# Loading the first feed-forward weights in smaller pieces, with GpSimd's v product among the loads

## The chip, the cores and the metric

The kernel runs on one core of a Trainium2 chip. The metric is the device time of one execution in microseconds (us). In the normal (fast) state, the granted TensorE clock was 0.99 to 1.00.

Engine names are those of the profile: PE is TensorE, PEld its weight loads, DVE VectorE, ACT ScalarE, POOL GpSimd, SP SyncE. L90 is line 90 of the kernel; the changed kernel's line numbers are one higher than those of the kernel before in most places.

## The reference, cut to what matters

A linear attention with decay (4 batches, 8 heads, 768 steps, head size 64) feeds a gated feed-forward layer:

```python
for t in range(S):
    state = gamma * state + einsum('bhd,bhe->bhde', k[:, :, t], v[:, :, t])
    y[:, :, t] = scale * einsum('bhd,bhde->bhe', q[:, :, t], state)
x = y.transpose(0, 2, 1, 3).reshape(B * S, H * D)          # 3072 x 512
gate = 1 / (1 + exp(-(x @ w_gate)))                        # w_gate, w_val: 512 x 1536
out = (gate * (x @ w_val)) @ w_out                         # w_out: 1536 x 512
```

The kernel cuts the steps into chunks of 128 and the 3072 rows of `x` into six tiles of 512. Of the feed-forward width, one "row block" is 128 of the 1536 columns of the gate and value weights.

## The kernel before

Nearly every load is issued by GpSimd, which also converts float32 to bfloat16 on the way. These loads pass through one queue in the order in which they are issued. The helpers for the weights, in which one call loads the gate and value weights of two row blocks:

```python
def load_gate_val(s):
    cols = slice(s * 256, (s + 1) * 256)
    for dst, w in ((wg, moe_w_gate), (wv, moe_w_val)):
        nc.gpsimd.dma_start(out=dst[:, :, cols],
                            in_=w.rearrange("(kk p) n -> p kk n", p=128)[:, :, cols])

def scale_run(a, eng):        # the "v product": v times its decay, bfloat16 out
    vsr[a] = const.tile([128, H, 2, D], BF16, name=f"vsr{a}")
    eng.tensor_tensor(vsr[a], runs(vr[a]), tabr[:, a]..., op=ALU.mult)
```

The order in which GpSimd gets its work is the order of these calls (all other engines' work is cut):

```python
vr[1] = load_run(v, 1, F32, "vr", nc.gpsimd)   # the "v run": chunks 2 and 3
...                                            # a mask
load_gate_val(0)                               # row blocks 0 and 1
load_gate_val(1)                               # 2 and 3
load_gate_val(2)                               # 4 and 5
scale_run(1, nc.gpsimd)                        # the v product, 1.9 us
...
extend_taby(3)                                 # a table, 1.0 us
for s in range(3, NFF // 2):
    load_gate_val(s)                           # row blocks 6 to 11
causal = ...; extend_taby(4); extend_taby(5)   # a mask and two tables
for s in range(4):
    load_out(s)                                # w_out in four parts
load_chunk(4)                                  # k, q, v of attention chunk 4
load_chunk(5)
...
```

`load_chunk(g)` issues k, q and v of a chunk. PE transposes k and q of chunks 4 to 7 itself when it reaches them; from chunk 8 a transposing load does it. PE's program is fixed, so a late load is a wait of PE.

Of the kernel before, what the change touches and what calls it, by code (L numbers as in the profile page):

```python
# [17 lines left out]
def kernel(  # L18
# [50 lines left out]
    def load_chunk(g):  # L69
        load_kq(g)  # L70
        load_v(g)
# [10 lines left out]
    wg = wpool.tile([128, KT, D_FF], BF16, name="wg")  # L82
    wv = wpool.tile([128, KT, D_FF], BF16, name="wv")
    wo = wpool.tile([128, NFF, D_MODEL], BF16, name="wo")

    def load_gate_val(s):
        cols = slice(s * 256, (s + 1) * 256)
        for dst, w in ((wg, moe_w_gate), (wv, moe_w_val)):
            nc.gpsimd.dma_start(out=dst[:, :, cols],
                                in_=w.rearrange("(kk p) n -> p kk n", p=128)[:, :, cols])  # L90

    def load_out(s):
        nc.gpsimd.dma_start(out=wo[:, s * 3:(s + 1) * 3, :],
                            in_=moe_w_out.rearrange("(n p) d -> p n d", p=128)[:, s * 3:(s + 1) * 3, :])
# [44 lines left out]
    def tab_y(c):  # L139
        first = c if c in taby else c - 1  # L140
        return taby[first][:, :, (c - first) * C:(c - first + 1) * C]
# [6 lines left out]
    def extend_taby(c):  # L148
        nc.gpsimd.tensor_tensor(tab_y(c), tab_y(c - 3), gup.unsqueeze(2).to_broadcast([128, NP, C]), op=ALU.mult)
# [5 lines left out]
    def bank(shape, dt=F32):  # L155
        return pf.tile(shape, dt, tag="ff", name="ff")
# [85 lines left out]
    def x_cols(t, kk, lo, hi):  # L242
        if hi - lo == 512:
            return xT[t][:, :, kk, :]
        half = lo // 256
        return xT[t][:, half, kk, lo - half * 256:hi - half * 256]
# [11 lines left out]
    def runs(t):  # L258
        return t.rearrange("x h (j d) -> x h j d", j=2)
# [19 lines left out]
    def scale_run(a, eng):  # L279
        vsr[a] = const.tile([128, H, 2, D], BF16, name=f"vsr{a}")  # L280
        eng.tensor_tensor(vsr[a], runs(vr[a]), tabr[:, a].unsqueeze(3).to_broadcast([128, H, 2, D]), op=ALU.mult)  # L281
# [20 lines left out]
    def inter_run(g, first=True):  # L302
        a, c = divmod(g, 2)
        if first:
            y[g] = bank([128, NP, C])
        if g > 0:
            for p in range(NP):
                nc.tensor.matmul(y[g][:, p, :], zbd[g - 1][:, p, :], qT[a][:, p, :, c * D:(c + 1) * D],
                                 start=(first and p == 0), stop=not first, skip_group_check=True)
# [25 lines left out]
    def sum_run(g):  # L335
        if g == 0:
            nc.vector.tensor_copy(new_za(g), zz[g])
        else:
            nc.vector.tensor_tensor(new_za(g), za[g - 1], zz[g], op=ALU.add)
# [42 lines left out]
    def up(t, n1, lo=0, hi=512, between=None):  # L382
        if t not in hT:
            hT[t] = ffn.tile([128, NFF, 512], BF16, tag="hT", name="hT", bufs=2)
        ps = []
        for w in (wg, wv):
            u = bank([128, 512])
            for kk in range(KT):
                nc.tensor.matmul(u[:, lo:hi], w[:, kk, n1 * 128:(n1 + 1) * 128], x_cols(t, kk, lo, hi),  # L389
                                 start=(kk == 0), stop=(kk == KT - 1))  # L390
            ps.append(u)
        if between:
            between()
        gs = ffn.tile([128, 512], F32, tag="gs", name="gs")
        nc.scalar.activation(gs[:, lo:hi], ps[0][:, lo:hi], AX.Sigmoid)  # L395
        nc.vector.tensor_tensor(hT[t][:, n1, lo:hi], gs[:, lo:hi], ps[1][:, lo:hi], op=ALU.mult)  # L396

    def up_columns(t, n1s, lo, hi, rows=1):
        if t not in hT:
            hT[t] = ffn.tile([128, NFF, 512], BF16, tag="hT", name="hT", bufs=2)  # L400
        n = hi - lo
        us = [bank([128, 512]), bank([128, 512])]
        for row in range(rows):
            for w, u in zip((wg, wv), us):
                for i, n1 in enumerate(n1s):
                    for kk in range(row * KT // rows, (row + 1) * KT // rows):
                        nc.tensor.matmul(u[:, i * n:(i + 1) * n], w[:, kk, n1 * 128:(n1 + 1) * 128],  # L407
                                         x_cols(t, kk, lo, hi), start=(kk == 0 and (rows == 1 or i == 0)),
                                         stop=(kk == KT - 1), skip_group_check=rows > 1)
        ps = [u[:, :len(n1s) * n] for u in us]  # L410
        gs = ffn.tile([128, 512], F32, tag="gs", name="gs")
        g = gs[:, :len(n1s) * n]
        nc.scalar.activation(g, ps[0], AX.Sigmoid)
        nc.vector.tensor_tensor(hT[t][:, n1s[0]:n1s[-1] + 1, lo:hi], g.rearrange("p (i n) -> p i n", n=n),  # L414
                                ps[1].rearrange("p (i n) -> p i n", n=n), op=ALU.mult)
# [18 lines left out]
    def keep_on(n, u):  # L434
        for _ in range(n):
            nc.tensor.matmul(u, ident, ident4, start=True, stop=True)  # L436
# [24 lines left out]
    for i in range(2):  # L461
        half = maskr[i * D:(i + 1) * D]
        nc.gpsimd.affine_select(half, half, pattern=[[-1, 2], [1, 2], [2, D]], base=0, channel_multiplier=-2,  # L463
                                compare_op=ALU.is_ge, fill=0.0)
    maskr2 = maskr.rearrange("x j i p -> x (j i p)").unsqueeze(1).to_broadcast([128, 2, 4 * D])
    load_gate_val(0)
    load_gate_val(1)
    load_gate_val(2)
    scale_run(1, nc.gpsimd)
    warm = bank([128, 4, 128])  # L470
    keep_on(9, warm)
    kT[0], qT[0], kT[1], qT[1] = (new_run_T() for _ in range(4))
# [22 lines left out]
    masks_run(1, 0)  # L495
    masks_run(1, 1)
    keep_on(2, warm)
    up_columns(0, range(0, 2), 0, 256)
    inter_run(2)
    state_run(1)  # L500
    sum_run(2)
    state_out(2, za[2])
    sum_run(3)
    extend_taby(3)
    for s in range(3, NFF // 2):
        load_gate_val(s)
    causal = const.tile([128, 128], F32, name="causal")
    nc.gpsimd.memset(causal, 1.0)
    nc.gpsimd.affine_select(causal, causal, pattern=[[1, 128]], base=0, channel_multiplier=-1,
# [1 line left out]
    causal4 = causal.unsqueeze(1).to_broadcast([128, NP, 128])  # L511
    extend_taby(4)
    extend_taby(5)
    for s in range(4):
        load_out(s)
    load_chunk(4)
    load_chunk(5)
    for load in (load_kq, load_v):
# [99 lines left out]
```

## Time and profile before

| | before |
|---|---|
| time, median (range), 3 runs | 230.01 us (229.79 to 231.38) |
| profiled execution | 229.69 us, span 228.0 |
| PE busy | 220.3 us, 97% of the span |
| v run of chunks 2 and 3 landed | 13.29 us after the start of the span |
| q of chunk 5 landed | 42.81 us |

PE is almost always busy, so a change can only gain where PE waits, and it loses wherever it makes PE wait longer. What GpSimd does (in its timeline the columns are start, duration, engine, line, operation, output<-input, and in brackets the idle time before it):

```profile
12.44 0.79 POOL L89 DMA_DIRECT2D wv<-in_moe_w_val_dram  x1
13.46 1.90 POOL L281 TENSOR_TENSOR vsr<-vr,tabr 128x1024 bf16<-128x1024 f32 x1 [0.23 <-ACT qkT L272]
15.32 1.04 POOL L149 TENSOR_TENSOR taby<-taby,gup 128x512 f32<-128x512 f32 x1
16.30 0.81 POOL L89 DMA_DIRECT2D wg<-in_moe_w_gate_dram  x1
```

From the end of the sixth weight issue (13.23) to 16.30, GpSimd issues nothing. Whether the queue notices depends on what is still in it. It did not notice here, as the stretches of two microseconds show (columns: stretch and length, busy time of PE, PEld, DVE, ACT and POOL with instruction counts, granted clock, DMA share, and GB/s in the last column):

```profile
16.00:18.00 2.00, 1.68 (x53) 1.39 (x56) 1.60 (x3) 0.93 (x2) 2.00 (x4) 1.00 1.43 193
18.00:20.00 2.00, 1.99 (x57) 1.45 (x44) 1.67 (x4) 1.19 (x3) 2.00 (x3) 1.00 1.44 199
20.00:22.00 2.00, 1.98 (x20) 1.62 (x18) 1.46 (x3) 1.26 (x4) 1.93 (x5) 1.00 1.46 195
...
24.00:26.00 2.00, 2.00 (x13) 1.04 (x11) 0.69 (x1) 0.81 (x2) 2.00 (x4) 1.00 1.48 204
```

(The DMA share is that of 16 engines; it exceeds 1 because the recorded times of an engine's packets overlap.)

### The profile page before, as it was taken

To read this page: it belongs to the slowest core of one execution; us is meant where nothing else is said; L and a number is where in the kernel's file an instruction comes from. 1 tells how busy PE (TensorE), PEld (TensorE's weight loads), DVE (VectorE), ACT (ScalarE), POOL (GpSimd) and SP (SyncE) were. 2 spreads that over 40 slices of the span, in tenths; PEclk is the share of its full clock that TensorE was granted. 3 is DMA by queue.
4 is the path that set the end of the run, shared out by engine and by line. 5 is a ranking of instruction groups with operands and counts; after the bars stand their busy time and mean duration, and the time that the engine had idled before them with its cause. 6 is when DMAs were issued, how large, how long until landed. Compare 5 with 4: busy or idle time off the path is not lost.

```text
span 228.0 us, 4533 instructions
## 1 busy us (share of the span) xinstructions
PE 220.3 (97%) x1815; PEld 119.4 (52%) x1815; DVE 117.9 (52%) x224; ACT 87.4 (38%) x162; POOL 78.6 (34%) x106
## 2 busy tenths in 40 slices
PE   4979999999999999999999999999999999999994
PEld 1558544557886455445445445454445454444444
DVE  5496433278877817359617358627267530343301
ACT  4695332563452422532522432523432412433221
POOL 7999956760814527090710090810000000000000
PEclk9999999999999999999999999999999999999999
DMA  7999999999999999899892499992410012100022
GB/s 138 214 183 196 198 205 197 177 256 205 141 155 65 171 186 146 189 140 155 78 185 84 110 136 151 100 155 92 113 26 3 0 49 92 46 0 0 4 92 92
DMA packets 77669, 28.09 MB, mean 123 GB/s; under 512 B 64208, under 2 KB 73296, under 8 KB 77648
## 3 DMA queue, kind: packets, MB, share of 16 engines
q0 software_dynamic: 55440, 16.78, 66.0%
q1 hardware_dynamic: 21536, 10.69, 24.4%
q10 hardware_dynamic: 672, 0.33, 0.5%
q8 instruction: 14, 0.23, 0.4%
q14 instruction: 7, 0.06, 0.1%
HBM read 28.31 MB, written 6.29 MB: 152 GB/s over the span
## 4 chain that ended last, share of the span: by engine, by line
PE 90%; DMA 5%; POOL 1%; ACT 1%; DVE 1%; issue 0%; DVEq 0%
PE ff L389 50%; PE ff L425 26%; PE ff L407 5%; DMA wv<-in_moe_w_val_dram 3%; PE ff L235 2%; PE ff L186 2%; DMA vr<-in_v_dram 2%; PE ff L198 1%; PE ff L444 1%; PE z L204 1%; PE ff L165 1%; DVE vsr L281 1%; ACT qkT L167 0%; POOL vr L79 0%; POOL maskr L463 0%; ACT zbd L210 0%
## 5 line engine op out<-in xcount | busy, mean ns | idle before, releaser
L396 DVE TENSOR_TENSOR hT<-gs,ff 128x512 bf16<-128x512 f32 (+1 forms) x70 | 44.7, 648 | 57.8 <-PE ff L389 53.4
L389 PE MATMUL ff<-xT,wg 128*128 128x512 bf16 (+1 forms) x280 | 67.7, 364 | 0.0
L389 PE MATMUL ff<-xT,wv 128*128 128x512 bf16 (+1 forms) x280 | 67.6, 364 | 0.0
L395 ACT ACTIVATE gs<-ff 128x512 f32<-128x512 f32 (+1 forms) x70 | 39.5, 567 | 68.0 <-PE ff L389 62.0
L425 PE MATMUL ff<-wo,hT 128*128 128x512 bf16 x276 | 62.2, 379 | 0.0
L389 PEld LDWEIGHTS <-wv 128*128 128x128 bf16 x280 | 27.3, 98 | 29.0 <-DMA wv<-in_moe_w_val_dram 0.3
L425 PEld LDWEIGHTS <-hT 128*128 128x128 bf16 x276 | 26.3, 98 | 30.5
L389 PEld LDWEIGHTS <-wg 128*128 128x128 bf16 x280 | 26.9, 98 | 27.8
L430 ACT COPY ob<-ff 128x512 f32<-128x512 f32 x23 | 13.5, 587 | 49.0 <-PE ff L425 44.8
L253 DVE TENSOR_TENSOR xT<-ff,taby 128x512 bf16<-128x512 f32 x20 | 12.9, 686 | 21.8 <-PE ff L235 21.8
L559 POOL COPY gate<-qkX 1x1 bf16<-1x1 bf16 x7 | 1.2, 178 | 57.7 <-DMA qkX<-qn 57.7
L66 POOL DMA_DIRECT2D kn<-in_k_dram x20 | 17.8, 892 | 6.2 <-DMA qkX<-kn 1.5
L61 POOL DMA_DIRECT2D vf<-in_v_dram x20 | 18.3, 913 | 2.3 <-DMA wo<-in_moe_w_out_dram 1.0
L67 POOL DMA_DIRECT2D qn<-in_q_dram x20 | 17.9, 893 | 2.1 <-DMA wo<-in_moe_w_out_dram 1.6
L210 ACT CAST zbd<-za 64x256 bf16<-64x256 f32 x38 | 15.4, 405 | 7.1 <-DVE za L222 3.1
L177 DVE TENSOR_TENSOR vs<-vf,tabv 128x512 bf16<-128x512 f32 x20 | 13.6, 687 | 7.4 <-DMA vf<-in_v_dram 7.4
L191 DVE TENSOR_TENSOR stA<-ff,causal 128x512 bf16<-128x512 f32 x20 | 13.6, 681 | 0.0
L192 DVE TENSOR_TENSOR stB<-ff,causal 128x512 bf16<-128x512 f32 x20 | 13.6, 681 | 0.0
L436 PE MATMUL ff<-ident 128*128 128x512 bf16 x15 | 5.8, 532 | 3.0 <-POOL ident masks.py:199 3.0
L407 PE MATMUL ff<-xT,wg 128*128 128x256 bf16 x56 | 7.3, 272 | 0.7 <-DMA wg<-in_moe_w_gate_dram 0.7
L407 PE MATMUL ff<-xT,wv 128*128 128x256 bf16 x56 | 7.3, 273 | 0.3 <-DMA wv<-in_moe_w_val_dram 0.3
L414 DVE TENSOR_TENSOR hT<-gs,ff 128x512 bf16<-128x512 f32 x7 | 4.7, 685 | 3.9 <-PE ff L407 2.8
(86 smaller groups left out, 150.9 us busy)
## 6 DMA issues: line engine op xcount, KB each, us to landing
out_dram<-ob SPq DMA_DIRECT2D x23, 256.0 KB, 2.0
vf<-in_v_dram POOLq DMA_DIRECT2D x20, 256.0 KB, 5.4
kn<-in_k_dram POOLq DMA_DIRECT2D x20, 128.0 KB, 5.3
qn<-in_q_dram POOLq DMA_DIRECT2D x20, 128.0 KB, 5.5
wg<-in_moe_w_gate_dram POOLq DMA_DIRECT2D x6, 256.0 KB, 8.0
wv<-in_moe_w_val_dram POOLq DMA_DIRECT2D x6, 256.0 KB, 8.5
wo<-in_moe_w_out_dram POOLq DMA_DIRECT2D x4, 384.0 KB, 10.4
kr<-in_k_dram POOLq DMA_DIRECT2D x2, 256.0 KB, 5.6
```

Source lines behind the costliest of these rows:

```text
L61: nc.gpsimd.dma_start(out=vf[g], in_=src(v, g))
L66: nc.gpsimd.dma_start(out=kn[g], in_=src(k, g))
L67: nc.gpsimd.dma_start(out=qn[g], in_=src(q, g))
L177: nc.vector.tensor_tensor(vs[g], vf[g], tabv[:, g % NCH, :].unsqueeze(2).to_broadcast([C, H, D]), op=ALU.mult)
L191: nc.vector.tensor_tensor(stA[g], sc[g][0], causal4, op=ALU.mult)
L192: nc.vector.tensor_tensor(stB[g], sc[g][1], causal4, op=ALU.mult)
L210: nc.scalar.copy(zbd[g % 4][half, :, half], z[half])
L389: nc.tensor.matmul(u[:, lo:hi], w[:, kk, n1 * 128:(n1 + 1) * 128], x_cols(t, kk, lo, hi), start=(kk == 0), stop=(kk == KT - 1))
L395: nc.scalar.activation(gs[:, lo:hi], ps[0][:, lo:hi], AX.Sigmoid)
L396: nc.vector.tensor_tensor(hT[t][:, n1, lo:hi], gs[:, lo:hi], ps[1][:, lo:hi], op=ALU.mult)
L407: nc.tensor.matmul(u[:, i * n:(i + 1) * n], w[:, kk, n1 * 128:(n1 + 1) * 128], x_cols(t, kk, lo, hi), start=(kk == 0 and (rows == 1 or i = ...
L425: nc.tensor.matmul(o, hT[t][:, n1, sm * 128:(sm + 1) * 128], wo[:, n1, :], start=(n1 == 0), stop=(n1 == NFF - 1))
```

## The change

The intent is that PE should not wait for 256 columns of gate weights when it needs only 128 to begin, and that the v product should run as soon as its data are there. The diff has five parts, named for later use: **W**, row blocks 0 to 3 come in eight loads of 128 columns instead of four of 256; **V**, the v product follows six of these small loads, and row block 3 and the gate half of row blocks 4 and 5 come behind it; **T**, the table now lies between the gate half and the value half of row blocks 4 and 5; **O**, w_out is issued ahead of the mask and the two tables; **U**, PE's first two row blocks are computed one after the other instead of together.

```diff
-    def load_gate_val(s):
-        cols = slice(s * 256, (s + 1) * 256)
-        for dst, w in ((wg, moe_w_gate), (wv, moe_w_val)):
+    def load_gate_val(s, width=256, which=(0, 1)):
+        cols = slice(s * width, (s + 1) * width)
+        for i in which:
+            dst, w = ((wg, moe_w_gate), (wv, moe_w_val))[i]
             nc.gpsimd.dma_start(out=dst[:, :, cols],
                                 in_=w.rearrange("(kk p) n -> p kk n", p=128)[:, :, cols])
 ...
-    load_gate_val(0)
-    load_gate_val(1)
-    load_gate_val(2)
+    for n1 in range(3):
+        load_gate_val(n1, 128)
     scale_run(1, nc.gpsimd)
+    load_gate_val(3, 128)
+    load_gate_val(2, which=[0])
 ...
-    up_columns(0, range(0, 2), 0, 256)
+    up(0, 0, 0, 256)
+    up(0, 1, 0, 256)
 ...
     extend_taby(3)
+    load_gate_val(2, which=[1])
     for s in range(3, NFF // 2):
         load_gate_val(s)
+    for s in range(4):
+        load_out(s)
     causal = const.tile([128, 128], F32, name="causal")
 ...
     extend_taby(4)
     extend_taby(5)
-    for s in range(4):
-        load_out(s)
     load_chunk(4)
     load_chunk(5)
```

## The prediction

> **What bounds the kernel now.** I read the page's first part and its chain of waits, then the waits of each engine, then the timeline around each wait that a load ends, and last the transfers one by one.
>
> The page says that TensorE (PE) is nearly always occupied:
>
> ```profile
> span 228.0 us, 4533 instructions
> PE 220.3 (97%) x1815; PEld 119.4 (52%) x1815; DVE 117.9 (52%) x224; ACT 87.4 (38%) x162; POOL 78.6 (34%) x106
> PE 90%; DMA 5%; POOL 1%; ACT 1%; DVE 1%; issue 0%; DVEq 0%
> ```
>
> The reader is to see that only about 8 us of the span aren't PE, and that DMA is the next name in the chain. The chain in order of time says where the change aims:
>
> ```profile
> 8.78 0.72 POOL wg L89
> 9.51 6.87 DMA wv<-in_moe_w_val_dram
> 16.42 1.05 PE ff L407 x8
> ```
>
> The timeline of PE there shows two stalls, at the first gate and at the first value weights:
>
> ```profile
> 13.77 0.61 PE L436 MATMUL ff<-ident 128*128 128x512 bf16 x2
> 15.05 1.05 PE L407 MATMUL ff<-xT,wg 128*128 128x256 bf16 x8 [0.68 <-DMA wg<-in_moe_w_gate_dram]
> 16.42 1.05 PE L407 MATMUL ff<-xT,wv 128*128 128x256 bf16 x8 [0.32 <-DMA wv<-in_moe_w_val_dram]
> ...
> 20.80 0.93 PE L407 MATMUL ff<-xT,wg 128*128 128x256 bf16 x7
> ```
>
> From 20.80 PE runs without a gap until the first attention chunk that is loaded normally. There the list of waits has one short line, and the timeline shows it at 42.85:
>
> ```profile
> 42.44 0.39 PE L165 MATMUL ff<-ident,kn 128*128 128x128 bf16 x4
> 42.85 0.23 PEld L165 LDWEIGHTS <-qn 128*128 128x128 bf16 x4 [0.20 <-DMA qn<-in_q_dram]
> ```
>
> That wait is only 0.2 us, but it means that PE and the queue of loads arrive at 42.85 together: **PE has no slack against the load of q for chunk 5**. I take this as the most important line for this change.
>
> **The queue behind it.** GpSimd issues every load of this stretch, and they land in order. By the view of transfers, wg issued at 8.74 lands 6.3 us later (15.0), wv issued at 9.51 after 6.9 (16.4), the next wg issued at 10.24 after 7.5 (17.7), the next wv issued at 10.97 after 8.0 (19.0): one lands each 1.3 us although each is under way 6 us and more. The q of chunk 5, issued at 32.45, takes 10.4 us and lands at 42.8. So the queue is backlogged from 9 us to 43 us, and a landing is set by what lies before it in the queue, not by its issue. GpSimd itself waits there for old transfers to finish (the profile has it idle before the v, k and q issues at 29.16 to 38.15, "<-DMA wg", "<-DMA wv", "<-DMA wo"), so an issue moved by one or two us is absorbed.
>
> The rate of that queue depends on the size of a piece. Three stretches of the DMA view, 6 to 7.5 us (k and q runs: pieces of 512 bytes of float32, 256 bytes as bf16), 17 to 20 us (weights by 256 columns: 1 KB, 512 bytes as bf16), 31.5 to 34 us (w_out: 2 KB, 1 KB as bf16):
>
> ```profile
> DMA packets 1040, 0.26 MB, mean 175 GB/s; under 512 B 1040, under 2 KB 1040, under 8 KB 1040
> DMA packets 1162, 0.59 MB, mean 197 GB/s; under 512 B 37, under 2 KB 1161, under 8 KB 1161
> DMA packets 525, 0.51 MB, mean 206 GB/s; under 512 B 23, under 2 KB 525, under 8 KB 525
> ```
>
> The sizes and rates are those of the bf16 side. Smaller pieces, lower rate: 175, 197, 206.
>
> **What the Trainium skill says.** "DMA: Bandwidth & Descriptors", section "Why small descriptors are slow (HBM only)", names a fixed overhead of about 3 cycles per packet beside one cycle per 32 bytes. By it a 512-byte read costs 16+3=19 and a 1 KB read 32+3=35 cycles, so two small ones cost 38/35 = 1.09 of a large one; the trace has 197/175 = 1.13. The direction agrees and the trace's size is a bit larger; I use the trace. The same page, section "Anatomy of one DMA — SWDGE (gpsimd) path", puts a fixed cost of about 2 us on each DMA, mostly completion latency; the 1.3 us between landings shows that in a full queue it overlaps, so I charge no such cost to the four extra DMAs. "Perfetto Trace Analysis", section "GPSIMD Engine Instruction", advises start-to-start spacing for GpSimd; so I take 0.75 us for one issue (8.74, 9.51, 10.24, 10.97), 1.86 for the v product (13.46 to 15.32) and 0.98 for the table extension (15.32 to 16.30).
>
> **The change part by part.**
>
> *Removed and added work.* PE's matmuls are the same in number and shape; two gate activations of 256 columns take the place of one of 512 (ACT: 2 x 0.38 instead of 0.60) and likewise on DVE (0.41 each instead of 0.69). Both are off PE's path. Four loads of 256 columns become eight of 128 (blocks 0 to 3).
>
> *Issue order.* Six small issues run from 8.74 to about 13.2, as the six large ones did; the v product waits for its data (it sat idle 0.23 until 13.46, when the v load of 6.60 + 6.7 had landed), so it stays at 13.46. Then come two small issues, one large gate issue (15.3 to 17.6), the table (to 18.6), and the rest. w_out goes out at about 23.7 to 26.7 as before, and the causal mask and two tables (some 2.6 us) now lie between w_out and chunk 4, whose k is issued at about 29.5 instead of 26.71. Because that k only lands at 26.71 + 12.1 = 38.8 behind w_out, this should cost nothing. No issue comes so late that the queue runs dry.
>
> *Gain at the front.* The first small gate tile should land near 14.4 and then one each 131,072 B / 175 GB/s = 0.75 us: 14.4, 15.1, 15.9, 16.6 for blocks 0 and 1, then 17.4, 18.1, 18.9, 19.6 for blocks 2 and 3. PE can begin block 0 at 14.85, once DVE has written its input (13.46 + 1.35), and ends block 1 at 16.6 + 0.44 = 17.0 instead of 17.3. From there DVE binds: its masks run until 17.1 whatever happens, then two products, two sums and the two y tiles, of which the last ended at 20.75 (20.01 + 0.74) before and let the next up columns begin at 20.80. I get 20.45 to 20.5 for that. So PE is **about 0.3 us earlier at 20.8**, and not the 1 us that the two stalls (0.68 + 0.32) suggest.
>
> *Cost in the queue.* Eight small loads take 8 x 0.749 = 5.99 us of the queue; four large ones take 4 x 262,144 B / 197 GB/s = 4 x 1.331 = 5.32. So everything behind them lands **about 0.67 us later**. Weights of blocks 4 and up don't notice: gate block 4 lands near 21.0 for a use at 24.0, and the last of w_out at 37.9 + 0.7 = 38.5 for a use at about 39.1. The q of chunk 5 does: 42.8 + 0.67 = 43.5, where PE now arrives at about 42.4.
>
> *Sum.* PE leaves that wait at 43.5 instead of 42.85, 0.65 us later; the 0.3 us won before only makes the wait longer. After it, PE is bound by itself or by things that follow from the same queue (the transposing loads of chunks 8 and 9, which wait for k at 51.2, used at 59.95), so the loss is carried to the end: 230.01 + 0.65 = 230.7. I shade this to 230.5 for the case that PE's front gain or the next loads recover part.
>
> **The rivals.** (1) *The front gain survives*: if the small loads run at the large ones' rate, q of chunk 5 lands at 42.8 as before; PE still can't pass it, so the gain is at most the 0.2 us of the present wait's neighbourhood, in truth about zero: 230.0. For it: both kinds read the same bytes. Against it: 175 against 197 GB/s in this trace, though from another tensor with another stride. (2) *The full 1 us is won*, 229.0: this needs chunk 5 to land earlier. Nothing in the diff removes bytes before it. (3) *The queue runs dry* because GpSimd stands in the v product and the table while only small loads are queued, or because chunk 4 is issued 2.8 us later: then 231.0 to 231.5. Against it: 6.3 to 12.1 us from issue to landing. (4) *New PSUM waits*: one by one, blocks 0 and 1 take four banks of the seven instead of two, so later banks wait for the masks; those end at 15.4 to 17.2, just ahead of their uses, so I give this at most 0.2 us at the front, which the wait at q hides.
>
> **Range and chances.** The mechanism's terms add to +0.65; rivals 1 and 3 give 0 and +1.3. Runs of before span 229.79 to 231.38. I take 230.5, with 229.7 to 231.3 for 8 times in 10. A change of 2% is 4.6 us, and nothing here is near it: faster 0.01, within 0.98, slower 0.01.
>
> **What would show it.** Right: the wait of PE for q of chunk 5 grows from 0.2 to about 1 us (0.65 + 0.3), its landing moves to about 43.5, the weights of blocks 0 to 3 land 0.75 us apart, and the first up columns of 256 to 512 start near 20.5. Wrong: q of chunk 5 lands at or before 42.8; or PE doesn't wait there and is still ahead at 50 us; or the stalls at 15.05 and 16.42 are simply moved to block 1 to 3 and 20.80 stays; or GpSimd's issues show idle DMA between 17 and 43 us.

## The result, and the profile after

| | before | changed |
|---|---|---|
| time, median (range) | 229.94 us (229.79 to 231.38), 6 runs | 233.10 us (232.28 to 233.66), 6 runs |
| ratio of fast runs | | 1.0118, 95% interval 1.0083 to 1.0153 |
| profiled execution | 229.69 us, span 228.0 | 233.66 us, span 232.0 |

A ratio is the mean time of one kernel's fast runs over that of the other's of the same rounds, so it is not quite the ratio of the medians quoted. The changed kernel is 3.2 us slower by the medians: within 2%, as the chances said, but outside the predicted range of 229.7 to 231.3. The profiled executions lie 4.0 us apart, because the one of the changed kernel is its slowest and the one of the kernel before is a fast one.

The first lines of the changed kernel's page, and its chain by engine:

```profile
PE 220.6 (95%) x1803; PEld 119.4 (51%) x1815; DVE 118.0 (51%) x225; ACT 87.6 (38%) x163; POOL 81.7 (35%) x110
PE 77%; DMA 13%; POOL 6%; issue 1%; ACT 1%; DVE 0%; POOLq 0%
```

PE has the same work (220.6 against 220.3 us busy) in a span 4.0 us longer, so the loss is waiting. DMA's share of the chain has gone from 5 to 13%, and GpSimd's from 1 to 6%. The chain in order of time says where (start, duration, what):

```profile
6.44 7.32 DMA vr<-in_v_dram
13.92 1.91 POOL vsr L282
...
18.07 1.07 POOL taby L150
...
24.24 11.86 DMA wo<-in_moe_w_out_dram
36.38 10.38 DMA qn<-in_q_dram
```

The chain now runs from the v run through the v product, GpSimd's issues and the table to a w_out load and the q of chunk 5. In the kernel before GpSimd was hardly in it. **On this chain it is GpSimd's own instruction time, from the v product to the w_out issue, that decides when the loads land.** Its timeline, to be read against the four lines above:

```profile
12.26 0.79 POOL L90 DMA_DIRECT2D wv<-in_moe_w_val_dram  x1
13.92 1.91 POOL L282 TENSOR_TENSOR vsr<-vr,tabr 128x1024 bf16<-128x1024 f32 x1 [0.87 <-DMA vr<-in_v_dram]
15.77 0.81 POOL L90 DMA_DIRECT2D wg<-in_moe_w_gate_dram  x1
...
18.06 1.07 POOL L150 TENSOR_TENSOR taby<-taby,gup 128x512 f32<-128x512 f32 x1
19.05 0.81 POOL L90 DMA_DIRECT2D wv<-in_moe_w_val_dram  x1
```

GpSimd stops issuing for 2.7 us (13.05 to 15.77) and again for 1.0 us at the table (18.06 to 19.05), against one stop of 3.1 us before (13.23 to 16.30). But now six *small* loads are queued at the first stop instead of six large ones. The rate of the DMA engines (last column) in the same stretches as above:

```profile
16.00:18.00 2.00, 1.77 (x49) 1.21 (x50) 2.00 (x5) 1.31 (x3) 2.00 (x3) 1.00 0.87 87
18.00:20.00 2.00, 1.93 (x66) 1.38 (x52) 1.58 (x4) 1.19 (x3) 2.00 (x4) 1.00 1.41 135
20.00:22.00 2.00, 1.71 (x14) 1.30 (x15) 1.42 (x3) 0.96 (x3) 2.00 (x3) 1.00 1.12 136
22.00:24.00 2.00, 2.00 (x21) 1.79 (x19) 0.67 (x2) 0.83 (x2) 2.00 (x4) 1.00 1.30 160
24.00:26.00 2.00, 2.00 (x16) 1.32 (x14) 0.74 (x2) 0.69 (x2) 1.83 (x3) 1.00 1.10 132
```

Where the kernel before had 193 to 204 GB/s, there are 87 to 160. The queue ran dry, and it did not come back to its full rate for some ten microseconds. "Dry" is meant of the 16 engines one by one: they finished the sixth load at 16.12 (the first), 16.88 (the median) and 18.33 us (the last), so most of them had nothing left to move before the next data came (17.8, estimated below).

The effect on the landings, from the records of each transfer (the time at which the last of the 16 DMA engines had finished its share):

| load | before | changed | later by | new in this step |
|---|---|---|---|---|
| v run | 13.29 | 13.75 | 0.46 | 0.46 |
| value of blocks 2 and 3 | 19.02 | 20.86 | 1.84 | 1.38 |
| value of blocks 4 and 5 | 21.73 | 24.92 | 3.19 | 1.35 |
| value of blocks 10 and 11 | 30.21 | 34.20 | 3.99 | 0.80 |
| last part of w_out | 37.86 | 41.85 | 3.99 | 0.00 |
| q of chunk 5 | 42.81 | 46.76 | 3.95 | -0.04 |

The first 0.46 is not the change's: the v run is issued before anything that the change touches, and it landed anywhere from 12.98 to 14.18 in the experiments. It may be a good part of the difference between the 4.0 us of the profiled pair and the 3.2 us of the medians. The rest arises between 14 and 34 us, and nothing is added after that.

On PE the lateness shows as waits in the new timeline at the end of the front and around 43 us:

```profile
20.29 0.61 PE L390 MATMUL ff<-xT,wg 128*128 128x256 bf16 x4 [0.36 <-DMA wg<-in_moe_w_gate_dram]
...
21.35 1.04 PE L408 MATMUL ff<-xT,wg 128*128 128x256 bf16 x8
...
41.90 0.81 PE L426 MATMUL ff<-wo,hT 128*128 128x512 bf16 x3 [1.14 <-DMA wo<-in_moe_w_out_dram]
...
43.79 0.40 PE L166 MATMUL ff<-ident,qn 128*128 128x128 bf16 x4 [0.58 <-DMA qn<-in_q_dram]
...
45.97 0.40 PE L166 MATMUL ff<-ident,kn 128*128 128x128 bf16 x4 [0.48 <-DMA kn<-in_k_dram]
46.80 0.40 PE L166 MATMUL ff<-ident,qn 128*128 128x128 bf16 x4 [0.44 <-DMA qn<-in_q_dram]
```

The up columns of 256 to 512, which began at 20.80, begin at 21.35. Then come four waits, 1.14 + 0.58 + 0.48 + 0.44 = 2.64 us, where the kernel before had one of 0.20. To follow the lateness, PE's weight loads can be paired one by one, since both kernels have 1815 of them: PE is 0.55 us later at 20.80 of the kernel before, 3.95 later at 42.85 (its q of chunk 5), and 3.98 later at the end. (The 3.40 added in between is more than the 2.64 of the matmuls' waits; PEld's own waits in that stretch, which partly coincide with them, add up to 4.4.) In the experiments below this is called PE's offset.

### The profile page after: what moved, and what is told of

Read it like the earlier page. It is cut to its first block, busy times and chain, and to the rows that moved or that the text cites. A ratio compares the mean times of both kernels' runs of the same rounds, so it can differ in the third digit from the quotient of the medians.

```text
span 232.0 us, 4529 instructions
## 1 busy us (share of the span) xinstructions
PE 220.6 (95%) x1803; PEld 119.4 (51%) x1815; DVE 118.0 (51%) x225; ACT 87.6 (38%) x163; POOL 81.7 (35%) x110
## 4 chain that ended last, share of the span: by engine, by line
PE 77%; DMA 13%; POOL 6%; issue 1%; ACT 1%; DVE 0%; POOLq 0%
PE ff L390 42%; PE ff L426 23%; DMA wo<-in_moe_w_out_dram 5%; DMA qn<-in_q_dram 4%; DMA vr<-in_v_dram 3%; PE ff L408 3%; PE ff L236 2%; PE ff L187 2%; POOL wg L90 2%; POOL wv L90 2%; PE ff L199 1%; PE ff L445 1%; PE z L205 1%; POOL vsr L282 1%; POOL qr L79 1%
## 5 line engine op out<-in xcount | busy, mean ns | idle before, releaser
L397 DVE TENSOR_TENSOR hT<-gs,ff 128x512 bf16<-128x512 f32 (+1 forms) x72 | 45.5, 641 | 58.1 <-PE ff L390 53.8
L390 PE MATMUL ff<-xT,wg 128*128 128x512 bf16 (+1 forms) x288 | 68.9, 362 | 1.1 <-DMA wg<-in_moe_w_gate_dram 0.6
L390 PE MATMUL ff<-xT,wv 128*128 128x512 bf16 (+1 forms) x288 | 68.8, 361 | 0.0
L396 ACT ACTIVATE gs<-ff 128x512 f32<-128x512 f32 (+1 forms) x72 | 40.2, 562 | 68.7 <-PE ff L390 62.6
L426 PE MATMUL ff<-wo,hT 128*128 128x512 bf16 x264 | 61.3, 379 | 2.1 <-DMA wo<-in_moe_w_out_dram 1.1
L390 PEld LDWEIGHTS <-wv 128*128 128x128 bf16 x288 | 28.0, 98 | 29.4 <-DMA wv<-in_moe_w_val_dram 0.6
L390 PEld LDWEIGHTS <-wg 128*128 128x128 bf16 x288 | 27.5, 98 | 29.9 <-DMA wg<-in_moe_w_gate_dram 1.0
L178 DVE TENSOR_TENSOR vs<-vf,tabv 128x512 bf16<-128x512 f32 x20 | 13.6, 687 | 10.4 <-DMA vf<-in_v_dram 10.4
L236 PE MATMUL ff<-stA,vs 128*64 128x128 bf16 x80 | 6.3, 222 | 0.0
L236 PE MATMUL ff<-stB,vs 128*64 128x128 bf16 x80 | 6.3, 222 | 0.0
L90 POOL DMA_DIRECT2D wv<-in_moe_w_val_dram x8 | 6.2, 779 | 0.0
```

Source lines behind the costliest of these rows:

```text
L90: nc.gpsimd.dma_start(out=dst[:, :, cols], in_=w.rearrange("(kk p) n -> p kk n", p=128)[:, :, cols])
L178: nc.vector.tensor_tensor(vs[g], vf[g], tabv[:, g % NCH, :].unsqueeze(2).to_broadcast([C, H, D]), op=ALU.mult)
L236: nc.tensor.matmul(y[g][i * D:(i + 1) * D, p, :], vs[g][:, 2 * p + i, :], st[:, p, :], start=(first and p == 0), stop=True, skip_group_che ...
L390: nc.tensor.matmul(u[:, lo:hi], w[:, kk, n1 * 128:(n1 + 1) * 128], x_cols(t, kk, lo, hi), start=(kk == 0), stop=(kk == KT - 1))
L396: nc.scalar.activation(gs[:, lo:hi], ps[0][:, lo:hi], AX.Sigmoid)
L397: nc.vector.tensor_tensor(hT[t][:, n1, lo:hi], gs[:, lo:hi], ps[1][:, lo:hi], op=ALU.mult)
```

## The experiments

The theory: **the queue runs dry**. An issue of these weights costs GpSimd 0.73 to 0.77 us whether the load is small or large, counted from one issue's start to the next (0.80 for the first behind a computation). A large load keeps the queue busy for 1.33 us, so each builds 0.6 us of reserve; a small one lasts 0.75 us and builds none. When GpSimd then stops for the v product, the small loads are used up, and every load behind them is late. The rival: **the small pieces themselves are the cost**, being slow for the DMA engines. A third: the other parts, **O and U**, cost something on PE or on later loads.

All kernels gave correct results. "Before" means runs of the kernel before on the same chip, medians 229.84 to 229.93. Each experiment has six runs, o1 and o3 have four. A landing or an offset comes from the one profiled execution of a run; the times are medians.

**e1_product_behind**: the changed kernel with the v product behind all loads that it had cut into.

```diff
-    for n1 in range(3):
+    for n1 in range(4):
         load_gate_val(n1, 128)
+    load_gate_val(2)
     scale_run(1, nc.gpsimd)
-    load_gate_val(3, 128)
-    load_gate_val(2, which=[0])
 ...
-    load_gate_val(2, which=[1])
```

> The changed kernel with its eight small loads, but all of them and both 256-column loads of blocks 4 and 5 issued ahead of GpSimd's v product, as the kernel before has its six. Theory 'the queue runs dry': the stretch of 16.5 to 19.5 us with 45 to 160 GB/s goes, the rate stays near 175 then 195 GB/s, q of chunk 5 lands near 43.5 to 44 instead of 46.75, and the time is 230.5 to 231.2 us. Rival 'small pieces are the cost': q of chunk 5 still lands past 46 and the time stays at 232.5 to 233.5.

Measured: 232.15 us (231.72 to 233.17), ratio 1.0094 [1.0068, 1.0120]; q of chunk 5 landed at 44.61. So it recovers a part, less than expected: both the time and the landing missed the range given for "runs dry", and the rival's too. The timeline of GpSimd and the rate in the last column tell why:

```profile
16.37 1.90 POOL L282 TENSOR_TENSOR vsr<-vr,tabr 128x1024 bf16<-128x1024 f32 x1
...
19.22 0.81 POOL L90 DMA_DIRECT2D wg<-in_moe_w_gate_dram  x1
```

```profile
16.00:18.00 2.00, 1.15 (x11) 0.75 (x10) 1.36 (x4) 0.66 (x2) 1.94 (x2) 1.00 1.76 180
20.00:22.00 2.00, 1.98 (x20) 1.52 (x19) 1.76 (x4) 1.35 (x5) 2.00 (x4) 1.00 1.03 129
```

The hole at 16 to 18 us is gone (180 instead of 87 GB/s), because no stop lies ahead of it. But eight small loads have built no reserve, so the product and the table, one after the other, make a new hole at 20 to 22 us. This run also gives the small pieces' own cost, since nothing interrupts them: from the v run's landing to the last of the eight it is 19.40 - 13.04 = 6.36 us, against 19.02 - 13.29 = 5.73 for the four large ones before. That is 0.63 us, and the whole loss is 3.2. The figure hangs on the engine that finishes last, though: by the mean of the 16 engines this pair shows no difference (5.71 and 5.70). Over the three runs in which eight small loads went through undisturbed (e1, e5, m1) and the eight with four large ones, the means are 6.11 and 5.51 us by the last engine and 5.68 and 5.29 by the mean of the engines. So the small pieces cost some 0.4 to 0.6 us.

**e2_wide_loads**: large loads again, in the new order, with the product and the table at the new places.

```diff
-    for n1 in range(3):
-        load_gate_val(n1, 128)
+    load_gate_val(0)
+    load_gate_val(1, which=[0])
     scale_run(1, nc.gpsimd)
-    load_gate_val(3, 128)
+    load_gate_val(1, which=[1])
```

> The changed kernel with the old 256-column loads in the new order: the same 768 KB (three loads instead of six) ahead of the v product, the fourth and the gate half of blocks 4 and 5 behind it, then the table, then the value half. Theory 'the queue runs dry': it still runs dry behind the v product, since only 4.0 us of work is queued there; q of chunk 5 lands near 45.5 to 46, the time is 231.8 to 233. Rival 'small pieces are the cost': no small piece is left, so the time is that of before, 229.8 to 230.3.

Measured: 232.40 us (231.55 to 234.50), ratio 1.0110 [1.0074, 1.0147]; q of chunk 5 at 44.24. With no small load at all, the median has most of the loss (2.5 of 3.2 us), so the size of the pieces is not its main cause: three large loads ahead of the product are too few as well. The landing of q was less late than expected (45.5 to 46); in the profiled execution, the slowest of the six, PE's offset was 1.4 us there and grew to 4.8 by the end, with 2.0 us of waits for later transposing loads. The time met its expectation, the place of the loss only partly.

**e3_filled**: one part of w_out, which is not urgent, goes ahead of the v product, to give the queue something to move.

```diff
     for n1 in range(3):
         load_gate_val(n1, 128)
+    load_out(0)
     scale_run(1, nc.gpsimd)
 ...
-    for s in range(4):
+    for s in range(1, 4):
         load_out(s)
```

> The changed kernel with the first w_out load (384 KB, 1.9 us of the queue) issued ahead of the v product instead of after the weights; same bytes in all. Theory 'the queue runs dry': the hole of about 1.3 us behind the six small loads is filled, q of chunk 5 lands near 43.5 to 44; value weights of block 3 come about 1 us later, so PE binds and the time is 230.8 to 231.6 us. Rival 'small pieces' and rival 'new order of PE or PSUM waits': no gain, 233 or more, since the front becomes later.

Measured: 231.30 us (230.61 to 234.22, this last one slow and left out of the ratio; the median of the five fast ones is 231.08), ratio 1.0057 [1.0024, 1.0090]; q of chunk 5 at 44.18. The bytes before q are the same and only their order differs, and half of the loss or a little more is gone. That is as "runs dry" has it. The rest can't all be put down to the queue: the filling load also delays row block 3, and PE's offset was 1.49 us already at 20.80 and 1.38 at q of chunk 5.

**e5_after_eight**: the v product after all eight small loads, the gate half of row blocks 4 and 5 still behind it.

```diff
-    for n1 in range(3):
+    for n1 in range(4):
         load_gate_val(n1, 128)
     scale_run(1, nc.gpsimd)
-    load_gate_val(3, 128)
     load_gate_val(2, which=[0])
```

> The changed kernel with the v product after all eight small loads, and nothing else moved: 6.0 us of work queued ahead of it instead of 4.5. Theory 'the queue runs dry': most of the hole goes; a hole of some 0.2 us behind the product and 0.4 us behind the table stay; q of chunk 5 lands near 44, time 230.8 to 231.6. Rival 'small pieces': 232.5 to 233.5.

Measured: 232.92 us (231.91 to 233.19), ratio 1.0111 [1.0085, 1.0137]; q of chunk 5 at 45.76. This expectation missed: I had counted two more small loads as reserve. By the theory's own arithmetic they add none, and the hole only moves. The run may show the change's hoped-for gain: with row block 3 no longer behind the product, PE was 0.54 us *earlier* than the kernel before at its 20.80. (Of the runs whose code is that of the kernel before up to there, f1, f2, g1, o1 and o3 lie from 0.15 earlier to 0.27 later and n1 1.79 later, so one execution proves little.) It was 2.95 us later at q of chunk 5 all the same.

**f1_late5 and f2_late10**: the kernel *before* with nothing changed but 5 or 10 idle fills on GpSimd (0.36 us each from start to start) ahead of the loads of row blocks 6 to 11. No load has another size, place in the queue or neighbour.

```diff
     extend_taby(3)
+    idle = const.tile([128, 256], F32, name="idle")
+    for _ in range(10):            # 5 in f1
+        nc.gpsimd.memset(idle, 0.0)
     for s in range(3, NFF // 2):
```

> The kernel before, its large loads untouched, with five idle fills of GpSimd (about 1.7 us) ahead of the loads of blocks 6 to 11. The queue still holds work for about 4.3 us when the first of them was issued at 16.30, and a load needs about 2 us from issue to its first byte, so 2.3 us are spare. Theory 'only a dry queue costs': nothing is lost, q of chunk 5 at 42.8, time 229.8 to 230.3. Theory 'a queue that is only thin is slow too': q of chunk 5 lands 0.5 to 1.5 us later and the time is 230.5 to 231.5.

> The same with ten fills (about 3.4 us), past the spare 2.3 us. Theory 'only a dry queue costs': about 1.1 us lost, q of chunk 5 near 43.9, time 230.9 to 231.3. Theory 'thin is slow too': 2 to 3 us lost, time 232 to 233, with single packets of over 0.2 us between 20 and 28 us as in the changed kernel. If neither loses, a late issue on GpSimd isn't what costs.

Measured: f1 231.05 us (230.27 to 231.92), ratio 1.0036 [1.0008, 1.0065], q of chunk 5 at 43.44. f2 233.25 us (232.09 to 234.29), ratio 1.0136 [1.0103, 1.0170], q at 44.82. **Ten fills reproduce the size of the whole loss in the kernel before**, though not its place: PE's offset was 2.0 us at q of chunk 5 and 3.1 at the end, the rest being waits for later transposing loads. Both runs speak for "a queue that is only thin is slow too" and against "only a dry queue costs". f2's GpSimd timeline, then its rates:

```profile
16.28 3.63 POOL L507 MEMSET idle<- 128x256 f32 x10
19.86 0.81 POOL L89 DMA_DIRECT2D wg<-in_moe_w_gate_dram  x1
```

```profile
20.00:22.00 2.00, 1.97 (x19) 1.62 (x17) 1.46 (x3) 1.24 (x4) 2.00 (x3) 1.00 0.55 60
22.00:24.00 2.00, 2.00 (x21) 1.79 (x19) 0.69 (x1) 0.92 (x2) 2.00 (x4) 1.00 1.32 174
24.00:26.00 2.00, 2.00 (x13) 1.05 (x11) 0.69 (x1) 0.82 (x2) 1.93 (x5) 1.00 0.94 110
```

The median engine finished the sixth load, the last one issued ahead of the stop, at 20.48 us. The next load, issued at 19.86, comes too late. The hole itself is in the line with 60 GB/s. But the line with 110, some four microseconds later, can't be a hole: by 24.38 GpSimd had issued all six large loads, which at 1.33 us each last 8 us from the time at which the first of them moves data. So a queue that has run dry costs more than the hole; it stays slow for a while. VectorE and ScalarE are no busier in that line (0.69 and 0.82 us) than in the kernel before (0.69 and 0.81). PE waited 0.47 us for k and 0.45 us for q of chunk 5.

f1 shows a loss with hardly a hole. Its first load behind the fills was issued at 18.43; with the 2.0 us that such a load needs (worked out below) it brings data at 20.4, when the median engine still had work until 20.80 and only the fastest, at 20.14, had none. Yet the rate fell to 157 GB/s later on:

```profile
22.00:24.00 2.00, 2.00 (x21) 1.80 (x19) 0.69 (x1) 0.92 (x2) 1.93 (x5) 1.00 1.29 157
```

So, as far as this run goes, a stop costs already when it only brings the queue near to empty.

**f3_order_only**: the kernel before with O and U alone.

```diff
-    up_columns(0, range(0, 2), 0, 256)
+    up(0, 0, 0, 256)
+    up(0, 1, 0, 256)
 ...
+    for s in range(4):
+        load_out(s)
     causal = const.tile([128, 128], F32, name="causal")
 ...
-    for s in range(4):
-        load_out(s)
     load_chunk(4)
```

> The kernel before with the two other parts of the change alone: blocks 0 and 1 by two single up calls, and w_out issued ahead of the causal mask and the two tables. Theory 'the cost is in the first loads': the time of before, 229.7 to 230.4, q of chunk 5 at 42.8. Rival 'PSUM waits or the moved w_out cost': 231 or more.

Measured: 230.07 us (229.33 to 230.54), ratio 0.9999 [0.9973, 1.0024]; q of chunk 5 at 42.37. The third theory falls: these parts together cost nothing.

**m1_e1_v_behind and g1_before_v_behind**: e1 and the kernel before, each with k and q of chunk 5 ahead of v of chunk 4 (and likewise for chunks 8 and 9), to give PE's tightest loads more room.

```diff
-    load_chunk(4)
-    load_chunk(5)
+    for g in (4, 5):
+        load_kq(g)
+    for g in (4, 5):
+        load_v(g)
 ...
-            load_chunk(8)
-            load_chunk(9)
+            for load in (load_kq, load_v):
+                load(8)
+                load(9)
```

> e1 (v product behind all first loads, 232.15 us, q of chunk 5 at 44.6 with PE only 0.63 us behind the kernel before when it gets there) with v of chunk 4 issued behind k and q of chunk 5, and v of chunk 8 behind k and q of chunk 9. Theory 'q of chunk 5 is the line that carries queue lateness to the end': k and q of chunk 5 land 1.3 us earlier, PE passes them 0.6 to 0.7 us late instead of 1.80, and the time falls to 230.5 to 231.2. If the time stays at 232, another load behind it binds as well.

> The kernel before with v of chunk 4 issued behind k and q of chunk 5, and v of chunk 8 behind k and q of chunk 9; nothing else. Theory 'q of chunk 5 is where PE meets the queue': the 0.2 us wait goes, q of chunk 5 lands near 41.5, PE is 0.2 us earlier at 43 us; the time is 229.4 to 229.9 against 229.84. If a later load takes its place, the time stays at 229.8 to 230.2.

Measured: m1 231.75 us (231.33 to 232.99), ratio 1.0082 [1.0055, 1.0109]; q of chunk 5 at 42.84 instead of e1's 44.61. The matmuls of PE no longer wait there (e1 had waits of 0.49 and 0.40 us). PE's offset at q fell from e1's 1.80 us to 0.37, but it was back to 1.65 at 73 us, with 0.9 us of waits for a transposing load. This confirms that q of chunk 5 is where PE first meets the queue. It also shows that the next meeting takes most of what this one gives up: the time fell by only 0.4 us against e1, less than the ranges of the two, and missed the range expected. g1 gave 229.79 us (229.39 to 230.08), ratio 0.9984 [0.9961, 1.0008]: q at 42.46, not the expected 41.5, since one DMA engine lagged (15 of 16 were done at 41.13); no wait of the matmuls at q, and no gain that the interval separates from zero. No version tried is shown to beat the kernel before.

**The slow return: n1_pairs, o1_late_out, o3_spaced.** Three more runs asked why the rate stays low after a hole. n1 and o3 are f2 with pauses after each pair of loads of row blocks 6 to 11: one fill of a single element in n1, two idle fills in o3. They test whether it is the issuing of several loads in one go that keeps a queue slow which has just run dry. o1 makes a hole later, with 17 fills (6.2 us) ahead of w_out in the kernel before, to test whether the slowness belongs to the time around 24 us.

```diff
     for s in range(3, NFF // 2):
         load_gate_val(s)
+        nc.gpsimd.memset(idle[0:1, 0:1], 0.0)        # n1
+        for _ in range(2): nc.gpsimd.memset(idle, 0.0)   # o3
 ...
     extend_taby(5)
+    for _ in range(17): nc.gpsimd.memset(idle, 0.0)  # o1 (without the fills of f2)
     for s in range(4):
         load_out(s)
```

> f2 (ten idle fills, q of chunk 5 at 44.8, 233.25 us) with a one-element fill of GpSimd behind each pair of weight loads. In the changed kernel and in e1, e2, e5, f1 and f2 alike the third load behind a computation of GpSimd lost another 0.7 to 1.2 us, though it had been issued 4.5 us and more before. If that comes from three and more loads issued in one go, no third one is left here: q of chunk 5 lands near 43.8 to 44.1 and the time is 232.0 to 232.6. If it comes from anything else (the time of day in the kernel, the engines after a dry queue), q of chunk 5 stays at 44.8 and the time at 232.8 to 233.5.

> The kernel before with seventeen idle fills of GpSimd (about 6 us) ahead of the four w_out loads, so that the queue runs dry near 29 us instead of 17 to 21. If an engine queue that ran dry always resumes slowly, the 31 to 36 us stretch stays under 180 GB/s for some us after the hole. If the slow resumption belongs to the stretch of 20 to 27 us and what runs there, the rate is back at 205 GB/s as soon as the hole ends, at about 31.5 us. q of chunk 5 near 44.5 to 45.5 and 231.5 to 233 us either way.

> f2 with two idle fills (0.7 us) behind each pair of weight loads: GpSimd then issues a pair (2.67 us of queue) each 2.2 us instead of each 1.5. If back-to-back issuing is what slows a nearly dry queue, the rate after the hole rises to about 195 GB/s and q of chunk 5 lands at 44 to 44.5, earlier than f2's 44.8. If a nearly dry queue only suffers from late issues, it lands later than in f2, 45 to 46.5, and the time is 233 to 234.5.

Measured: n1 233.05 us (232.32 to 234.75), ratio 1.0133 [1.0098, 1.0169], the same time as f2; q of chunk 5 at 45.78. o3 234.71 us (233.72 to 236.31), ratio 1.0206 [1.0153, 1.0259]: the dip at 24 to 26 us was milder (175 GB/s against f2's 110), but the later loads came so late that a second hole opened at 30 to 32 us (139); q landed at 45.39, as expected for loads that only suffer from late issues. o1 234.88 us (234.51 to 236.08), ratio 1.0220 [1.0171, 1.0269], with q of chunk 5 at 46.27, both later than expected; its rates around the hole, in the last column:

```profile
30.00:32.00 2.00, 2.00 (x11) 0.88 (x9) 0.96 (x2) 0.60 (x1) 2.00 (x3) 1.00 0.28 16
32.00:34.00 2.00, 2.00 (x12) 0.88 (x9) 0.84 (x2) 0.61 (x2) 2.00 (x4) 1.00 1.02 162
34.00:36.00 2.00, 2.00 (x11) 0.94 (x10) 0.69 (x1) 0.87 (x2) 2.00 (x3) 1.00 1.22 191
```

The kernel before moved 206 GB/s with the same loads of w_out. In o1 the hole reaches to about 32.5 us and so lowers the 162; after it come 191, and 179 in the two microseconds that follow. So there is a slow return after this hole too, wherever it lies, though a milder one than in f2. It is visible in single packets: between 20 and 28 us, 32 packets of the changed kernel took over 0.2 us (the median packet 0.06), 25 in f2 and 23 in f1, and none in the kernel before or in f3.

What makes them slow stays open. In the changed kernel, e1, e2, e5, f1 and f2 the third load behind the last stop lost more than its neighbours. By the median engine it came 2.39 us behind the second in f2, against 1.33 for a large load in a full queue. In n1, in which no more than two loads are issued in one go, it was 2.07, which speaks against that idea. In o3, with longer pauses, it was 1.45: there the loss at that place is nearly gone. That speaks for the idea, but it is one execution, and o3's second hole hides what it was worth in time.

## Why the prediction was wrong, step by step

**What bounds the kernel, and where PE meets the queue: right.** q of chunk 5 was the line to watch. Its load took 10.4 us from issue, PE waited for it, and the lateness there (3.95 us) was still there at the end (3.98). f1 confirms that there is no slack: a landing only 0.6 us later (in its profile) cost 1.2 us by the medians and 0.8 by the ratio.

**"Eight small loads take 8 x 0.749 ... everything behind them lands about 0.67 us later": right in sign and about in size.** The runs give some 0.4 to 0.6 us: the small loads took 1.07 to 1.11 times as long (5.68/5.29 and 6.11/5.51). The 1.09 that the prediction worked out from the figure of the Trainium skill is an estimate, and it lies in this range; the 1.13 of its other tensors lies above it.

**"No issue comes so late that the queue runs dry": this is the step that failed.** The working behind it was the 6 to 12 us from issue to landing in the kernel before. That number says how long the queue is when *large* loads fill it, and the change replaces the loads that filled it. The other support, that GpSimd "itself waits there for old transfers" so that a later issue "is absorbed", was read outside the stretch that counts: the first such wait stands at 29.16, and none lies between the issues of 8.74 and 28 us. What should have been compared is the time at which the queue empties with the time at which the next load brings data. The median DMA engine finished the sixth load at 20.65 us in the kernel before and at 16.88 in the changed one. A load needs about 2 us from its issue until the engines move its data (my estimate: the load issued at 15.77 had landed on its first engine at 18.55, less 0.75 for its own move). So the first load behind the stop brings data at 16.30 + 2.0 = 18.3 before, which leaves a reserve of 2.3 us, and at 15.77 + 2.0 = 17.8 in the changed kernel, 0.9 us after the queue was empty. The prediction had most of the durations for this sum: 0.75 us per issue, 0.75 us per small load, 1.86 and 0.98 us for the stops. It used the issue costs for the *order* and never for a balance of filling against emptying. Two things it had not measured: the 2.0 us, and that the median engine is done well ahead of the last one, by which it counted landings (16.88 against 18.33 us here, the prediction having 18.1 for this load). By the last engine alone the sum shows a thin queue and not yet a dry one.

The prediction also drew on the Trainium skill, "DMA: Bandwidth & Descriptors", "Anatomy of one DMA — SWDGE (gpsimd) path", for a fixed cost of about 2 us per DMA, and charged nothing because it overlaps in a full queue. That holds while the queue is full, and that was the condition to be checked. What stood bare after a stop was the 2.0 us *ahead of* the data that is estimated above. The page puts most of its 2 us behind the data, a part which no run here shows apart.

**Rival 3 (the queue runs dry) named the mechanism and mis-sized it**: 231.0 to 231.5 was given, about 1.0 to 1.5 us, against a measured 3.2. The arithmetic just made gives a hole of 0.9 us, and the rest has two sources. One is the second stop, the table at 18.06, which meets a queue with nothing in reserve. The other is the slow return after a hole. f2 supports the latter: its arithmetic, 19.86 + 2.0 against 20.48, gives a hole of about 1.4 us, and PE was 2.0 us late at q and 3.1 at the end of its profiled execution. How much of the changed kernel's 1.35 and 0.80 us in the table of landings is the second stop and how much the slow return is not separated by these runs.

**The gain at the front: plausible, but lost to V.** The prediction gave 20.45 to 20.5 for the start of the next up columns; it was 21.35. The cause is that row block 3 lies behind the v product, and its two small loads landed at 20.25 and 20.86 instead of 18.9 and 19.6, late by the same failed step. e5, which moves these two loads forward, had PE 0.54 us earlier than the kernel before, in one execution. The gain could not have survived the wait at q of chunk 5, as the prediction said.

**w_out at 38.5 for a use at 39.1: wrong as a consequence.** It landed at 41.85, and PE waited 1.14 us for it. **The later issue of chunk 4 and the PSUM banks (rival 4) cost nothing: right**, by f3.

**Its own sign of being wrong came true:** "GpSimd's issues show idle DMA between 17 and 43 us" is what the 87 GB/s at 16 to 18 us and the rates behind it show.

**The range** was too narrow for a reason that can be named: its upper end allowed rival 3 only at its small size, and a rival whose size is not worked out deserves a wider one.

## What to carry to other kernels

A queue of loads has a balance: each load adds the time that its bytes last and takes the time that its issue costs, and a small load may add nothing (here 0.75 us gained and 0.75 spent). Before cutting loads into smaller pieces or moving other work of the issuing engine among them, work out how long the queue lasts at each stop of that engine, leave some reserve beyond that (f1 lost time with 0.4 us left by the median engine), and put a large load that nobody needs soon ahead of the stop. A latency from issue to landing, read in a kernel whose queue is full, says nothing of a kernel whose queue is being emptied.

## What the Trainium skill lacked or had wrong

- "DMA: Bandwidth & Descriptors", section "Anatomy of one DMA — SWDGE (gpsimd) path", calls descriptor generation small and says that many can be emitted before the cost shows up. Here each issue of such a load took GpSimd 0.73 to 0.80 us, for loads of 128 columns and of 256 alike. That is as long as the queue needed to move a small one (0.75 us), so a run of small loads could build no reserve. No page has the resulting rule of reserve.
- The same page, section "Latency and other measured facts", gives about 1 us to the first byte on this path and doesn't say from when. Here it was an estimated 2.0 us from the start of an issue and 1.2 us from its end (15.77 + 0.81, estimated first data at 17.8), and 2.2 us in f2 (19.86, estimated first data at 23.37 - 1.33 = 22.04).
- None has it: after the queue had run dry, its rate stayed at 87 to 160 GB/s for 10 us in the changed kernel, and in f2 it fell again to 110 GB/s two microseconds after it had been back at 174, with six large loads issued. f1 fell to 157 GB/s with hardly a hole. The cause is open.
